# A block of output products that keeps its sums in a retired token buffer, with the scalings of v moved into it

## The chip, the cores and the metric

One core of one Trainium2 chip runs the kernel. Times are device microseconds (us) of one launch; the profile is one more execution, recorded by the hardware profiler, with a span of its own.

## The reference, cut to what matters

```python
# q, k, v: (8, 8, 576, 64); x: (4608, 512); w1, w2: (512, 1024); w3: (1024, 1024); w_out: (1024, 512)
scores = q @ k.T / 8                       # per batch and head
ret = scores * gamma_h ** (i - j), i >= j  # causal decay, gamma_h = 1 - 2 ** (-5 - h)
x = ret @ v                                # heads side by side: (8 * 576, 512)
out = ((x @ w1) * (x @ w2)) @ w3 @ w_out   # float32
```

## The kernel before, in words

Attention is done in chunks. Four pairs of batches times five chunks (64, then four of 128 positions) make 20 steps g. A step scales q and v by the decay (`scale`, `scale_blocks`), transposes q and k (`front` on TensorE, `front_blocks` on VectorE), makes scores (`score`), adds to a running state (`state`) and multiplies with v (`pv`), which leaves x transposed, in tiles of 2 x 192 tokens called xT; there are 12 such tiles m.

The feed-forward part works with seven products in the place of eight (Strassen's scheme). `up` makes a and b of 384 tokens, and their product goes into a tile named `ab` (128 x 16 x 192 values, two buffers in the pool `ffn`). w3 and w_out are multiplied into w3o once. `down` takes a pair of tiles of 128 tokens and multiplies them with w3o: products 1, 7, 2, 6, 5, 4, 3 in this order, four matmul steps each; product 2 goes on in the PSUM bank of product 1, and product 3 in that of product 5.

The order of every engine's work is written out by hand. A `down` block does this (lines of the kernel before):

- It takes an output tile `ot` (L640), 128 x 2 x 2 x 256 values, from a pool with ONE buffer. So the first write of a block waits until the stores of the block that last had this buffer have landed.
- After product 1, ScalarE copies the bank into `ot` (L679); product 2 waits for this copy, since it goes on in that bank. Once `open_second` has been run, the copy goes to another buffer (`cc` or `ra` in the profile).
- After product 6 VectorE adds into `ot` (L695), and ScalarE copies the finished first quadrant (L696). `plus` (L649) adds products 7, 5, 4 and 3. Product 3 waits for the addition of product 5.
- `put` and `store` (L723) send finished rows to HBM, from ScalarE's queue. A DMA issue stands in ScalarE's order like any other instruction.
- After each addition `plus` runs one entry of the list `spread` (sums of weights and their sends to HBM) or, when that is empty, of `pieces` (sums of tokens for the next part), and, except after that of product 3, one entry of the list `aside`. With `ahead`, a block puts the three sums S3, S2 and S1 of the next block (L614, L618, L620) at the end of `aside`.

Around the change three such blocks follow each other. Block 1 is `down((1,0),(1,1))`, in the last step of the loop `first_pair` and after it. Then come `pv(2*NC-1)`, the load and the scaling of v for the step after it (`scale(g + 1, "v", True)`: eight ScalarE instructions, L202, one for each head), and `open_first`, which starts the next sends and loads of weight forms. Block 2 is `down((2,2),(3,2))`, then `open_second` is run, and block 3 is `down((3,0),(3,1))`, with the scaling of q in `aside`. Then `front(10)` transposes k and q (L218), with copies on ScalarE (L221), `state` (L255) and `score` (L233) follow, and a long stage of two-level products (`up2`, L1053) begins. It reads weight forms from three buffers `ra`, filled from `kept` tensors in HBM (L954), which the sends (L895, L898, L901) had written in pieces during the three blocks. The first two fills of `ra` are issued by SP.

Transfers issued by SP and ScalarE share eight completion counters. In the built program, an issue first waits until the transfer that last used the same counter has landed. So a store on ScalarE can wait for a send of SP.

Of the kernel before, what the change touches and what calls it, by code (L numbers as in the profile page):

```python
# [8 lines left out]
F32 = mybir.dt.float32  # L9
# [10 lines left out]
def kernel(  # L20
# [16 lines left out]
    B, H, S, D = q.shape  # L37
    DM = H * D
    DF = moe_w3.shape[0]
    CV = 512  # L40
    P = 128
# [12 lines left out]
    TB = S // NB  # L54
    NT = 2 * TB // P
    KD = DM // P
    KF = DF // P
# [6 lines left out]
    ffn = ctx.enter_context(tc.tile_pool(name="ffn", bufs=2))  # L64
# [6 lines left out]
    pools = {}  # L71
# [123 lines left out]
    def scale(g, nm, scalar=False, engine=nc.gpsimd):  # L195
        c = g % NC
        sz = sizes[c]
        t, gam = live[nm, g], {"q": gq, "v": gk}[nm]
        t = t[:sz].rearrange("p (b h) d -> p b h d", b=2)
        if scalar:  # L200
            for h in range(H) if scalar is True else scalar:
                nc.scalar.mul(t[:, :, h, :], t[:, :, h, :], gam[:sz, c, h:h + 1])  # L202
            return
        engine.tensor_tensor(
            out=t, in0=t, in1=gam[:sz, c].unsqueeze(1).unsqueeze(3).to_broadcast([sz, 2, H, D]), op=ALU.mult)
# [366 lines left out]
    aside, owed, spread, beside, loads = [], [], [], [], []  # L572
    g = 0
# [31 lines left out]
    def pair_of(x, y):  # L605

        if (x, y) not in pairs:
            X, Y = tokens(*x), tokens(*y)
            a = {"A11": X[:, :NP], "A12": X[:, NP:], "A21": Y[:, :NP], "A22": Y[:, NP:],
                 "S3": Y[:, :NP], "S4": X[:, NP:]}  # L610

            def sums(nm):
                if nm == "S3":
                    nc.vector.tensor_tensor(out=a["S3"], in0=a["A11"], in1=a["A21"], op=ALU.subtract)  # L614
                elif nm == "S2":
                    forms = pools["forms"].tile([P, 2, NP, P], F32, tag="forms", name="forms")
                    a["S1"], a["S2"] = forms[:, 0], forms[:, 1]
                    nc.vector.tensor_tensor(out=a["S2"], in0=a["A22"], in1=a["S3"], op=ALU.subtract)  # L618
                else:
                    nc.vector.tensor_tensor(out=a["S1"], in0=a["S2"], in1=a["A11"], op=ALU.add)  # L620
                done.append(nm)

            done = []
            pairs[x, y] = a, done, [lambda nm=nm: sums(nm) for nm in ("S3", "S2", "S1")]
        return pairs[x, y]

    def ahead(x, y, n=3):
        todo_sums = pair_of(x, y)[2]
        for _ in range(min(n, len(todo_sums))):
            aside.append(todo_sums.pop(0))  # L630

    def down(x, y, then=None, last=False):
        a, done, left = pair_of(x, y)
        second = "first" in live
        early = second or last or g >= 2 * NC - 1
        ahead(x, y)
        while len(done) < (1 if second else 3):
            aside.pop(0)()
        ps = {}
        ot = pools["ot"].tile([P, 2, 2, DM // 2], F32, tag="ot", name="ot")  # L640

        def product(nm, A, B, on=None):
            ps[nm] = ps[on] if on else acc.tile([P, DM // 2], F32, tag="acc", name="po")
            for f in range(NP):
                nc.tensor.matmul(ps[nm], a[A][:, f, :], live["W"][B][:, f, :], start=(f == 0 and not on),  # L645
                                 stop=(f == NP - 1), skip_group_check=True)

        def plus(nm, to, sb):
            nc.vector.tensor_add(ot[:, to[0], to[1]], ps[nm], ot[:, sb[0], sb[1]])  # L649
            if spread:  # L650
                spread.pop(0)()
            elif pieces:
                pieces.pop(0)()
            if early and aside and nm != 3:
                aside.pop(0)()

        def put(m, t, row, half=slice(0, 2)):

            i, n = every[m]
            r0 = t * P  # L660
            while r0 < (t + 1) * P:
                b = r0 // TB
                e = min((b + 1) * TB, (t + 1) * P)
                r = (2 * i + b) * S + n * TB + r0 - b * TB
                stores.append((out[r:r + e - r0, half.start * DM // 2:half.stop * DM // 2],
                               ot[r0 - t * P:e - t * P, row, half].rearrange("p h d -> p (h d)")))
                r0 = e
            if not keep_stores and not second:
                store()

        C11, C12, C21, C22 = (0, 0), (0, 1), (1, 0), (1, 1)
        product(1, "A11", "B11")
        first = ot[:, 0, 0]
        if second and not steps[0]:
            first = live["spare"]
        elif second:
            first = live["first"].pop(0)
            live["first"].append(first)
        nc.scalar.copy(first, ps[1])  # L679
        if second:  # L680
            store()
            finish()
            if steps[0] and sent[0] < steps[0] + 3:
                next_forms()
        product(7, "S3", "T3")
        if second:
            multiply()
        while len(done) < 3:
            aside.pop(0)()
        if then:  # L690
            ahead(*then)
        product(2, "A12", "B21", on=1)
        nc.vector.tensor_tensor(out=a["S4"], in0=a["A12"], in1=a["S2"], op=ALU.subtract)
        product(6, "S2", "T2")
        nc.vector.tensor_add(ot[:, 0, 1], ps[6], first)  # L695
        nc.scalar.copy(ot[:, 0, 0], ps[2])  # L696
        if early:
            put(*x, 0, slice(0, 1))
            store()
        plus(7, C21, C12)  # L700
        product(5, "S1", "T1")
        plus(5, C22, C21)
        product(4, "A22", "-T4")
        plus(4, C21, C21)
        put(*y, 1)
        if second:
            store()
        product(3, "S4", "B22", on=5)
        while aside and not early:
            aside.pop(0)()  # L710
        plus(3, C12, C12)
        put(*x, 0, slice(1 if early else 0, 2))
        if last:
            store()
        while aside:
            aside.pop(0)()
# [3 lines left out]
    def store(engine=nc.scalar):  # L720
        while stores:

            engine.dma_start(*stores.pop(0))  # L723
# [125 lines left out]
    ahead((2, 0), (2, 1), 1)  # L849
    up(0, 2, NQ - 1)  # L850
    down((2, 0), (2, 1), ((0, 0), (0, 1)))
    carry(2, 2)
    weights_part.close()
# [6 lines left out]
    keep_stores.clear()  # L860
    store()
    todo = [(down, (0, 0), (0, 1)), (down, (0, 2), (1, 2))]


# [85 lines left out]
    def next_forms(engine=nc.gpsimd):  # L950
        n = sent[0]
        if n < 14 * len(groups):
            nm = NAMES.index(OPERANDS[order[n % 7]][0])
            engine.dma_start(ring[n % 3], kept[n % 14 // 7][nm])  # L954
            sent[0] += 1
# [57 lines left out]
    def finish():  # L1013
        while behind:
            behind.pop(0)()

    def multiply(most=2 * len(order)):
        while results and most:
            gr, h, f, b, z, s = results.pop(0)
            m = groups[gr][s]  # L1020
            if ("ab", *every[m]) not in live:
                live["ab", *every[m]] = ffn.tile([P, 2 * KF, TB], F32, tag="ab", name="ab")
            ab = live["ab", *every[m]].rearrange("p (q i) t -> p q i t", i=4)[:, 2 * h:2 * h + 2, 2 * f + b, :]
            v = z.rearrange("p (m s) w t -> p m s w t", s=2)[:, :, s]
            nc.vector.tensor_mul(ab, v[:, :, 0, :], v[:, :, 1, :])  # L1025
            if s == 0:
                free.append(z)
            most -= 1

    def up2(gr, n):  # L1030
# [88 lines left out]
        behind.append(rest)  # L1119

    real = (up, up2, down)

    def add_group(gr):
# [4 lines left out]
    def work(n):  # L1128
        while n > 0 and todo:
            fn, *args = todo.pop(0)  # L1130

            nxt = next((x for x in todo if x[0] in real), None)
            if nxt and nxt[0] is down:
                if fn is down:
                    args.append(nxt[1:])
                else:
                    ahead(*nxt[1:], 1 if fn is up2 else 3)
            if g == G and not todo:
                fn(*args, last=True)
            else:  # L1140
                fn(*args)
            n -= 1
            while todo and todo[0][0] not in real:
                todo.pop(0)[0]()

    g = NC
# [49 lines left out]
    g = 2 * NC - 1  # L1196
# [3 lines left out]
    pv(g)()  # L1200
    load(g + 2, "v", nc.scalar)
    load(g + 2, "k")
    scale(g + 1, "v", True)
    open_first()
    token_forms(0)

    g = 2 * NC
    work(1)
    aside.append(lambda: scale(g, "q", True))
    work(1)  # L1210
# [55 lines left out]
    g = G  # L1266
# [44 lines left out]
```

## Time and profile before

| what | value |
|---|---|
| median of 3 runs | 835.94 us (835.65 to 836.12) |
| the profiled execution: its own time | 834.5 us |
| the profiled execution: span | 832.8 us |
| TensorE busy in the span | 814.8 us, 98% |
| VectorE, ScalarE, GpSimd busy | 546.3, 291.6, 216.3 us |
| window 335 to 365 us, TensorE busy | 26.59 of 30 us |
| window 335 to 365 us, DMA | share 1.10, 304 GB/s |
| window 400 to 800 us, TensorE busy | 398.04 of 400 us |

In the views, PE is TensorE, PEld its weight loads, DVE VectorE, ACT ScalarE, POOL GpSimd, SP SyncE; a q after an engine's name is its queue, where DMAs are issued. A line of the timeline gives the start, the length, the engine, the line of the kernel, the operation with tiles out<-in, the number of instructions, and in brackets the idle time before it with what ended it. A DMA share of one means that 16 DMA engines had packets all the time (packets overlap, so it can be a little over one).

### The profile page before, as it was taken

What the parts mean: (1) busy time and instruction counts of PE and PEld (TensorE: products, weight loads), DVE (VectorE), ACT (ScalarE), POOL (GpSimd) and SP (SyncE); (2) the same over time, 40 slices, a digit from 0 to 9 for tenths busy, and PEclk for the clock granted to TensorE, in tenths of its full rate; (3) what the DMA queues carried; (4) which work ended last, traced back from release to release, by engine and by line L of the source; (5) the groups of instructions that cost most, each with busy time, mean ns of one, the idle gap of its engine ahead of it and who ended that gap; (6) DMA issues with size and microseconds to landing.
All of it is one profiled execution on the core that took longest, in us unless ns stands there. A gap on an engine that the chain in (4) does not pass through costs nothing.

```text
span 832.8 us, 15818 instructions
## 1 busy us (share of the span) xinstructions
PE 814.8 (98%) x6117; PEld 733.5 (88%) x6117; DVE 546.3 (66%) x962; ACT 291.6 (35%) x609; POOL 216.3 (26%) x247
## 2 busy tenths in 40 slices
PE   7999999999999999999999999999999999999998
PEld 7888999644888998789999889998889998899987
DVE  4899999992554558754657755677745667646653
ACT  4787566581111010245443024341034331033300
POOL 1000000001103262005556005565006460045600
PEclk9999999999999999999999999999999999999999
DMA  9995464436045568998886447978245453145311
GB/s 195 228 215 138 78 153 127 123 105 112 3 80 130 86 175 276 286 282 209 202 227 184 100 85 205 232 232 222 56 92 180 162 191 114 37 150 215 138 30 46
DMA packets 197485, 126.96 MB, mean 152 GB/s; under 512 B 157849, under 2 KB 179097, under 8 KB 197409
## 3 DMA queue, kind: packets, MB, share of 16 engines
q1 hardware_dynamic: 168560, 50.40, 29.4%
q0 software_dynamic: 11824, 63.31, 23.4%
q10 hardware_dynamic: 17024, 12.23, 5.3%
q8 instruction: 48, 0.79, 0.4%
q14 instruction: 29, 0.23, 0.1%
HBM read 103.62 MB, written 22.28 MB: 151 GB/s over the span
## 4 chain that ended last, share of the span: by engine, by line
PE 81%; DVE 7%; DMA 5%; SPq 3%; issue 2%; ACT 2%; POOL 0%; ACTq 0%; DVEq 0%
PE po L645 21%; PE up L1053 17%; PE up L528 14%; PE seed L1053 13%; PE ps L477 7%; PE xps L299 3%; PE sc L233 3%; PE xps L274 1%; DMA out_dram<-ot 1%; PE st L255 1%; SPq L171 1%; DMA bl_k<-in_k_dram 1%; DVE ab L1025 1%; PE tp L218 1%; DMA kept<-wA 1%
## 5 line engine op out<-in xcount | busy, mean ns | idle before, releaser
L645 PE MATMUL po<-w3o,ab 128*128 128x256 f32 x552 | 125.4, 381 | 3.3 <-DVE ot L649 2.4
L645 PEld LDWEIGHTS po<-w3o,ab 128*128 128x128 f32 x552 | 103.6, 190 | 20.4 <-DVE ot L649 4.8
L1058 POOL TENSOR_TENSOR cc<-cc 128x384 f32<-128x384 f32 x112 | 109.3, 1002 | 3.8 <-ACT cc L1076 2.4
L1065 DVE TENSOR_TENSOR cc<-seed,cc 128x384 f32<-128x384 f32 x88 | 48.7, 553 | 69.1 <-PE seed L1053 60.1
L1053 PE MATMUL up<-xT,ra 128*128 128x192 f32 x384 | 73.6, 328 | 0.4 <-DMA ra<-kept 0.4
L181 POOL TENSOR_TENSOR bl_q<-bl_q,gqs 128x512 f32<-128x512 f32 (+1 forms) x26 | 26.0, 1020 | 184.1 <-DMA bl_q<-in_q_dram 180.5
L528 PE MATMUL up<-xT,wA 128*128 128x192 f32 x384 | 70.8, 328 | 0.3 <-ACT xT L306 0.3
L533 DVE TENSOR_TENSOR c<-up,c 128x384 f32<-128x384 f32 x80 | 44.0, 551 | 38.9 <-PE up L528 38.6
L1065 DVE TENSOR_TENSOR cc<-up,cc 128x384 f32<-128x384 f32 x88 | 48.5, 551 | 29.8 <-PE up L1053 21.8
L236 DVE TENSOR_TENSOR pm<-sc,mask 128x512 f32<-128x512 f32 (+1 forms) x80 | 45.3, 628 | 33.4 <-PE sc L233 33.3
L1053 PEld LDWEIGHTS up<-xT,ra 128*128 128x128 f32 x384 | 63.7, 190 | 1.7 <-DMA ra<-kept 0.7
L645 PE MATMUL po<-wB,forms 128*128 128x256 f32 x288 | 65.1, 379 | 0.0
L528 PEld LDWEIGHTS up<-xT,wA 128*128 128x128 f32 x384 | 63.3, 190 | 1.8 <-issue 0.7
L645 PEld LDWEIGHTS po<-wB,forms 128*128 128x128 f32 x288 | 54.7, 190 | 7.4
L1072 ACT COPY seed<-up 128x384 f32<-128x384 f32 x56 | 25.9, 463 | 100.1 <-PE up L1053 59.2
L954 POOL DMA_DIRECT2D ra<-kept x53 | 29.9, 565 | 117.7 <-PE seed L1053 88.5
L477 PE MATMUL ps<-wo,w3T 128*128 128x512 f32 x128 | 55.1, 592 | 0.0
L1053 PE MATMUL up<-ra 128*128 128x192 f32 x288 | 54.8, 326 | 0.0
L1053 PE MATMUL seed<-e,ra 128*128 128x192 f32 x256 | 50.9, 329 | 0.0
L477 PEld LDWEIGHTS ps<-wo,w3T 128*128 128x128 f32 x128 | 24.3, 190 | 30.1 <-issue 29.7
L1053 PEld LDWEIGHTS up<-ra 128*128 128x128 f32 x288 | 48.1, 190 | 0.1
L528 PE MATMUL up<-T,wS 128*128 128x192 f32 x256 | 46.7, 326 | 1.3 <-ACT e L395 1.3
(129 smaller groups left out, 1463.8 us busy)
## 6 DMA issues: line engine op xcount, KB each, us to landing
ra<-kept POOLq DMA_DIRECT2D x53, 896.0 KB, 5.1
raw<-in_moe_w_dram SPq DMA_DIRECT2D x72, 128.0 KB, 3.0
out_dram<-ot ACTq DMA_DIRECT2D x50, 128.0 KB, 2.3
bl_q<-in_q_dram SPq DMA_DIRECT2D x192, 32.0 KB, 3.3
bl_k<-in_k_dram SPq DMA_DIRECT2D x136, 32.0 KB, 3.2
raw<-in_moe_w_dram SPq DMA_DIRECT2D x16, 256.0 KB, 6.1
ld_k<-in_k_dram SPq DMA_DIRECT2D x8, 512.0 KB, 6.3
raw<-in_moe_w_out_dram SPq DMA_DIRECT2D x32, 128.0 KB, 2.7
```

The costliest lines, as they stand in the source:

```text
L181: nc.gpsimd.tensor_tensor(out=part, in0=part, in1=gqs[:, :, n0:n0 + n].unsqueeze(3).to_broadcast([P, NP, n, BL]), op=ALU.mult)
L233: nc.tensor.matmul(sc[j][:sz, p, :sz], kT[hs, b, p, :sz], qT[hs, b, p, :sz], start=True, stop=True)
L236: nc.vector.tensor_mul(pm[:sz, b, j, :, :sz], sc[j][:sz, :, :sz], mask[:sz, :sz].unsqueeze(1).to_broadcast([sz, NP, sz]))
L477: nc.tensor.matmul(ps, live["w3T", ft][:, g, :], live["wo"][:, g, :], start=(g == 0), stop=(g == KF - 1))
L528: nc.tensor.matmul(ps[:, w, :], a[:, w, r, :], b[:, r, :], start=(new and w == r == 0), stop=(w == r == 1), skip_group_check=True)
L533: nc.vector.tensor_add(c[:, to], ps, c[:, sb])
L645: nc.tensor.matmul(ps[nm], a[A][:, f, :], live["W"][B][:, f, :], start=(f == 0 and not on), stop=(f == NP - 1), skip_group_check=True)
L954: engine.dma_start(ring[n % 3], kept[n % 14 // 7][nm])
L1053: nc.tensor.matmul(ps[:, w, :], weight_of(slot, a, w), B[b], start=(new and w == 0), stop=True, skip_group_check=True)
L1058: nc.gpsimd.tensor_tensor(out=o, in0=o, in1=i, op=ALU.add)
L1065: nc.vector.tensor_add(c[:, j], ps, with_add[:, j])
L1072: nc.scalar.copy(p6, p1)
```

## The change

Two edits. The output tile of block 2, the one called with x == (2, 2), is no longer taken from the one-buffer pool; a buffer of the pool `ffn` with the tag `ab` is taken, under the name `spare`, and its first 2048 values a partition are used in the shape of `ot`. With the order in which the two `ab` buffers are handed out, it is the one that held the tokens of block 1. The scaling of v for step 10 is no longer ahead of block 2; it is put into `aside` in two halves of four heads, so that it runs after the additions of products 7 and 5 of block 2.

```diff
@@ down
-        ot = pools["ot"].tile([P, 2, 2, DM // 2], F32, tag="ot", name="ot")
+        if x == (2, 2):
+
+            ot = ffn.tile([P, 2 * KF, TB], F32, tag="ab", name="spare").rearrange("p f t -> p (f t)")
+            ot = ot[:, :2 * DM].rearrange("p (r c d) -> p r c d", r=2, c=2)
+        else:
+            ot = pools["ot"].tile([P, 2, 2, DM // 2], F32, tag="ot", name="ot")
@@ main order
     load(g + 2, "k")
-    scale(g + 1, "v", True)
     open_first()
     token_forms(0)
 
     g = 2 * NC
+    aside.extend(lambda j=j: scale(g, "v", range(j, j + H // 2)) for j in (0, H // 2))
     work(1)
     aside.append(lambda: scale(g, "q", True))
     work(1)
```

## The prediction

> **What bounds the kernel now.** The page comes first: is there one engine that sets the time?
>
> ```profile
> span 832.8 us, 15818 instructions
> PE 814.8 (98%) x6117; PEld 733.5 (88%) x6117; DVE 546.3 (66%) x962; ACT 291.6 (35%) x609; POOL 216.3 (26%) x247
> ```
>
> TensorE is busy for 98% of the span, so only its idle time can be won, and only where the change acts. I then read TensorE's timeline for the three blocks.
>
> ```profile
> 338.97 1.99 PE L645 MATMUL po<-w3o,carry 128*128 128x256 f32 x8 [1.40 <-ACT ot L679]
> ...
> 346.66 1.99 PE L645 MATMUL po<-w3o,carry 128*128 128x256 f32 x8 [0.52 <-DVE ot L649]
> ...
> 360.67 1.99 PE L645 MATMUL po<-w3o,ab 128*128 128x256 f32 x8 [1.31 <-DVE ot L649]
> ```
>
> Three stalls: product 2 of block 2 (1.40 us), product 3 of block 2 (0.52), product 3 of block 3 (1.31), together 3.23 us. That is all this stretch has to give. Why they are there, the timelines of VectorE and ScalarE tell.
>
> ```profile
> 357.59 0.42 DVE L695 TENSOR_TENSOR ot<-po,cc 128x256 f32<-128x256 f32 x1 [2.68 <-DMA out_dram<-ot]
> ```
>
> ```profile
> 336.21 2.45 ACT L202 ACTIVATE ld_v<-ld_v,gk 64x128 f32<-64x128 f32 x8
> 338.56 0.36 ACT L679 COPY ot<-po 128x256 f32<-128x256 f32 x1
> ...
> 362.85 1.12 ACTq L723 DMA_DIRECT2D out_dram<-ot  x2
> 364.01 0.65 ACT L221 COPY kT<-tp 128x256 f32<-128x256 f32 x2 [1.34 <-PE tp L218]
> 364.54 0.67 ACT L221 COPY qT<-tp 128x256 f32<-128x256 f32 x2
> ```
>
> Stall one: the copy L679 stands behind eight scalings of v. Stall three: block 3's first addition waits until block 2's last store has landed, since both use the one `ot`. The last three lines matter for what comes next: ScalarE issues block 3's two stores of the lower rows and only then copies kT and qT, which the scores need. Last, the DMA, in the table of windows:
>
> ```profile
> 335.00:365.00 30.00, 26.59 (x158) 21.92 (x157) 21.89 (x38) 8.22 (x26) 0.03 (x1) 1.00 1.10 304
> ```
>
> The share is 1.10 over the whole stretch: the transfers are saturated beside all this.
>
> [...] the stores of L723 at 362.85 show 1.12 us, but ScalarE's copies are held until these are out, at 363.97. [...] for SP's queue: sends issued at 350.93, 354.63, 357.57 and 359.69 landed after 7.2, 7.8, 5.2 and 4.6 us, so at 358.2, 362.4, 362.8 and 364.3, in order. [...] the granted clock is 1.00 in all windows, and no gap of this stretch exceeds 1.40 us.
>
> **Part 1, the scalings moved.** Removed ahead of L679: eight of L202, 2.45 us together. The copy of product 1 now goes to the spare buffer, needs no store to have landed, and follows the xT copies that end at 336.33. It ends near 336.7, before product 7 ends at 337.55. So product 2 starts near 337.55: stall one is gone, minus 1.40. The scalings come after ScalarE's first store of block 2. In the built program this store waits for the counter of the v load issued at 335.36, which takes 7.7 us, so until 343.0; the scalings then run to 346. Their reader, `state`, was at 363.7. Cost nothing, under a cover of 17 us; without it 2.45 us. The load of v isn't moved.
>
> **Part 2, `aside` reordered.** Two scalings now stand ahead of the sums S3, S2, S1. VectorE's order becomes: addition of 7, weight sums (1.22 + 0.95), additions of 5 and 4, three token sums (2.01), S3, addition of 3, two sums of 0.95, S2, S1. Before, S3 (0.69) stood ahead of the addition of 5. From L695 near 341.4: the addition of 5 starts near 344.2 and ends at 344.6; product 4 ends at 344.7. So stall two is gone, minus 0.52. S3 ends near 347.9 and the addition of 3 at 348.2, when product 7 of block 3 wants S3 and its bank (product 1 of block 3 ends near 348.4). S2 and S1 end at 350.6 and 351.2, wanted at 352.1 and 353.9. Cost nothing; slack 0.2 us at the tightest.
>
> **Part 3, the buffer.** Block 3 takes `ot` again, whose last stores are those of block 1; they were out before the copy at 338.56. So L695 of block 3 no longer waits 2.68 us. It follows product 6, at 354.1; the addition of 5, behind sums of 0.95 and 1.02, ends near 357.0, and product 4 ends at 357.5. Stall three is gone, minus 1.31. The spare buffer had block 1's tokens, all read when product 3 of block 1 ended, at 331.0, and in the built program the copy into it waits for product 1 alone; it is next written by products near 385, with its stores landed. Cost nothing. No transfer and no arithmetic is added or taken away.
>
> **Sum up to here:** block 3 ends at 362.6 - 3.2 = 359.4.
>
> **Part 4, what is late next.** TensorE transposes k and q (1.2 us) and does `state` (1.15), to about 361.8. Then scores need qT. Before, scores began at 364.99, 0.98 us after the kT copies began (364.01), with TensorE fed until then. ScalarE reaches the stores of the lower rows earlier now, but these wait for counters. In the built program of before the two wait for the fifth and the sixth send of the second half's weight forms, in the new one for the fourth and the fifth. The fifth is the one issued at 357.57 and landed 5.2 us later, at 362.8. It stands in SP's queue behind 2.7 MB or more (a fill of `ra`, 896 KB; four sends of 256 KB, one of 768 KB), all under a saturated DMA, so an earlier issue gains it nothing. What changes its landing: block 3's stores are earlier [...]. The first was under way before as well; one of 128 KB is new ahead of it. At 304 GB/s that is 0.43 us, an upper bound; the lower is nothing, or a gain of 0.2 if the earlier stores of block 2 fill the one weak microsecond at 345 (DMA share 0.78, 211 GB/s in the table of windows). I take +0.2: 363.0. Then 0.1 to the issue, about 0.5 for it (1.12 for two), and kT begins near 363.6 in the place of 364.01. Gain 0.4, bounds 0.0 to 0.7. The scores then begin at 364.6 and TensorE idles about 2.8 us ahead of them: of the 3.2, 2.8 come back as one new wait.
>
> **After that.** The second step of the long stage needs the second fill of `ra`, issued at 364.51 when the last send of weights had landed, and in 5.1 us later, at 369.6. TensorE wanted it at 371.5, so it had 1.9 us of cover. With one to three stores (128 to 384 KB, 0.4 to 1.3 us at 304 GB/s) now ahead of the last send it comes at 370.0 to 370.9, and is wanted at 371.1: it just holds, and would stop any gain above 0.6 to 1.9. From 365 to the end TensorE's waits add up to 2.0 us, none on absolute times; counters and orders are the same again after the first block loads, so the 0.4 goes through.
>
> **Sum.** Span 832.8 - 0.4 = 832.4; with the 1.7 around it 834.1 against the profiled 834.5. The median shown is 1.44 above that execution: 835.94 - 0.4 = 835.5 us. Within 0.2% (1.67 us), about what a measurement of this kernel can tell from no change.
>
> **Rivals.**
> (a) *No wait takes the stalls' place*: the sends land early enough. 835.94 - 3.2 = 832.7. For it: ScalarE is idle and the sums are done. Against it: the share of 1.10. Chance 0.05.
> (b) *The counter wait ends earlier, the second fill of `ra` is the next limit*: gain 0.8 to 1.9, so 834.0 to 835.1; I take 1.4, 834.5. It needs the fifth send in by 362. [...] Against: the order of landing. Chance 0.16, a third of it past 0.2%.
> (c) *Slower: [...] halves the clock.* Place: between `state` and the scores. [...] Chance 0.10.
> (d) *The change doesn't do what it says*, since the buffer handed out is still read: the time of before, 835.9. Against it is the end of its readers at 331.0 (part 3). Chance under 0.01.
>
> **Numbers.** Main case 0.69, own range 835.2 to 836.0. Faster by over 0.2%: 0.05 from (a), 0.05 from (b), 0.03 for a landing of sends that I have wrong by more than its bounds: 0.13. Slower by over 0.2%: 0.06 from (c), [...] 0.04 for a wait not seen here: 0.10. Within: 0.77. For 8 in 10 the range takes most of (b) and the mild half of (c): 834.1 to 836.9.
>
> **What would show it.** Right: no stall ahead of products 2 and 3 in blocks 2 and 3; L695 of block 3 near 354; one TensorE gap of 2 to 3 us ahead of L233, on ScalarE's qT or kT copy; these right behind the stores of L723, which wait for a send of weights landed near 363. Wrong: the copies come by 362, and the gap is small (a, b); or PEclk falls under 1 after 364 (c); or one of the three stalls stays.

## The result and the profile after

The changed kernel takes 837.08 us (median of 22 runs, 836.24 to 841.32), the kernel before, run beside it, 835.66 us (22 runs): a ratio of 1.0018, 95% interval 1.0010 to 1.0027. The forecast was 835.5. The time went 1.4 us up and not 0.4 down, and lies 0.2 us over the top of the range. Single runs of one kernel spread over 4 us or so here. TensorE's clock has a part in that: the two longest runs of the changed kernel, 841.32 and 841.11 us, have the lowest mean clock, 0.990. The mean granted clock was 0.996 or less in 15 of the 22 runs of the changed kernel, and in 21 of 128 runs of the kernel before that were taken beside the experiments; it was 0.999 or more in none of the 22, and in 72 of the 128. A mean doesn't tell where the clock fell. The profiled execution of the changed kernel took 836.71 us and has a mean clock of 0.996.

The page after: span, engines, and the row of the granted clock in 40 slices.

```profile
span 835.0 us, 15819 instructions
PE 816.9 (98%) x6117; PEld 736.2 (88%) x6117; DVE 544.9 (65%) x962; ACT 291.6 (35%) x609; POOL 216.3 (26%) x247
PEclk9999999999999999989999999999999999999999
```

One slice has an 8 in the clock's row; before there was none. The rest of the kernel is the same, so the stretch of the three blocks is looked at again. TensorE's timeline (lines after block 1 have moved down by five in the code):

```profile
337.89 1.89 PE L650 MATMUL po<-w3o,carry 128*128 128x256 f32 x8
...
344.89 1.99 PE L650 MATMUL po<-w3o,carry 128*128 128x256 f32 x8
...
357.08 1.89 PE L650 MATMUL po<-w3o,ab 128*128 128x256 f32 x8
358.90 0.71 PE L218 MATMUL tp<-ident,ld_k 64*128 64x64 f32 x8
359.45 0.66 PE L218 MATMUL tp<-ident,ld_q 64*128 64x64 f32 x8
360.04 1.15 PE L255 MATMUL st<-ld_v,ld_k 64*64 64x64 f32 x32
364.54 1.97 PE L233 MATMUL sc<-qT,kT 64*64 64x64 f32 x32 [3.36 <-ACT qT L221]
366.44 2.93 PE L1046 MATMUL seed<-w3o,ident 128*128 128x384 f32 x4
```

The first three lines had brackets before (1.40, 0.52, 1.31 us); now they have none, and block 3 ends at 358.9. More was won than these 3.23 us. Two windows, the first of the kernel before and the second of the changed one, go from the first product of block 2 to the first transpose (columns: window, length, then busy time and count of PE, PEld, DVE, ACT, POOL, then granted clock, DMA share and GB/s):

```profile
333.85:362.59 28.74, 25.44 (x114) 20.87 (x113) 20.70 (x35) 7.15 (x22) 0.00 (x0) 1.00 1.11 303
334.33:358.90 24.57, 24.57 (x114) 20.98 (x113) 20.89 (x35) 7.36 (x22) 0.00 (x0) 1.00 1.12 295
```

The same matmuls are through in 24.57 us in the place of 28.74, so 4.17 us sooner: 3.30 us of idle time are gone, and 0.87 us of what was shown as busy. Then TensorE waits 3.36 us for qT. Before, the scores, the matmuls after them (into a tile named `seed`) and the first matmuls of the second step of the long stage were

```profile
364.99 1.15 PE L233 MATMUL sc<-qT,kT 64*64 64x64 f32 x32
366.07 1.56 PE L1041 MATMUL seed<-w3o,ident 128*128 128x384 f32 x4
...
371.53 0.81 PE L1053 MATMUL up<-xT,ra 128*128 128x192 f32 x4
```

Now the scores take 1.97 us for the same 32 matmuls, and the four into `seed` 2.93. What ScalarE did meanwhile:

```profile
360.79 2.73 ACTq L728 DMA_DIRECT2D out_dram<-ot  x2
363.56 0.65 ACT L221 COPY kT<-tp 128x256 f32<-128x256 f32 x2 [8.15 <-DMA out_dram<-ot]
364.09 0.39 ACT L221 COPY qT<-tp 128x256 f32<-128x256 f32 x1
364.35 0.35 ACTq L959 DMA_DIRECT2D ra<-kept  x1
```

ScalarE does no work for 8.15 us, in part because it stands at two stores; the second is held until 363.05. In the built program it waits there for the fifth send of weights, which SP issued at 357.93 and whose last write landed at 363.03. The table of windows, with the same columns, tells why the work after the gap is slow:

```profile
360.00:362.00 2.00, 1.18 (x34) 1.01 (x32) 1.86 (x6) 0.00 (x0) 0.58 (x1) 1.00 1.08 385
362.00:364.00 2.00, 0.00 (x0) 0.00 (x0) 0.00 (x0) 0.44 (x2) 0.00 (x0) 0.99 1.11 355
364.00:366.00 2.00, 1.46 (x28) 1.46 (x30) 0.31 (x1) 1.33 (x4) 0.00 (x0) 0.50 1.05 280
366.00:368.00 2.00, 2.00 (x13) 1.28 (x10) 1.18 (x4) 0.00 (x0) 0.00 (x0) 0.50 0.86 330
368.00:370.00 2.00, 2.00 (x6) 1.39 (x5) 0.00 (x0) 0.00 (x0) 0.00 (x0) 0.50 1.05 438
370.00:372.00 2.00, 2.00 (x12) 1.93 (x11) 0.00 (x0) 0.94 (x2) 0.00 (x0) 0.81 0.73 159
```

The clock is at half from just before 364 to nearly 371, and at once when the work comes back. From the scores to the first matmul of the second step of the long stage it is 9.36 us (364.54 to 373.90), before 6.54 (364.99 to 371.53): 2.82 us. Block 2 began 0.48 us later in this execution than in the one of before (334.33 against 333.85), so the scores came 0.93 us earlier than before, counted from there. 2.82 - 0.93 = 1.9 us are lost at the second step; with the 0.48 of the later start that is 2.4, and the spans differ by 2.2.

There is a second thing, in the view of single DMA issues. These are the two fills of `ra` for the second and the third step, of the changed kernel (columns: KB each, us to landing):

```profile
ra<-kept ACTq DMA_DIRECT2D x1, 896.0 KB, 8.5
ra<-kept SPq DMA_DIRECT2D x1, 896.0 KB, 8.6
```

Before, SP's fill was out 0.48 us ahead of ScalarE's and was in after 5.1 us, at 369.6. Now the two start at 364.38 and 364.35, and both land near 373. The second step is wanted at 373.9 with the clock as it is, so here nobody waits. With the full clock it would have been wanted near 371 (an estimate: 364.54 and the 6.54 us of before). So there are two suspects: **the clock** (theory A) and **the fills that share the transfers** (rival B).

### The profile page after: what moved, and what is told of

It reads as the page before. It is cut to its first block, busy times and chain, and to the rows that moved or that the text cites. A ratio compares the mean times of both kernels' runs of the same rounds, so it can differ in the third digit from the quotient of the medians.

```text
span 835.0 us, 15819 instructions
## 1 busy us (share of the span) xinstructions
PE 816.9 (98%) x6117; PEld 736.2 (88%) x6117; DVE 544.9 (65%) x962; ACT 291.6 (35%) x609; POOL 216.3 (26%) x247
## 4 chain that ended last, share of the span: by engine, by line
PE 87%; DMA 5%; DVE 4%; SPq 2%; issue 1%; ACT 1%; POOL 0%; ACTq 0%; DVEq 0%
PE po L650 23%; PE up L1058 17%; PE up L528 14%; PE seed L1058 13%; PE ps L477 7%; PE sc L233 4%; PE xps L299 4%; PE xps L274 2%; PE st L255 1%; DMA ld_q<-in_q_dram 1%; PE tp L218 1%; SPq L171 1%; DMA raw<-in_moe_w_dram 1%; DMA bl_k<-in_k_dram 1%; DVE ab L1030 1%
```

## The experiments

Ten kernels, each timed beside the kernel before, whose median was 835.73 to 835.91 us then. The ratio is not the quotient of the two medians and can differ from it by 0.1% (the buffer alone).

| run | median us | ratio to before (95%) | wait ahead of scores in the profile, us | halved clock after 360 in the profile |
|---|---|---|---|---|
| changed kernel | 837.08 | 1.0018 (1.0010 to 1.0027) | 3.36 | 6.8 us |
| buffer alone | 836.72 | 1.0002 (0.9990 to 1.0015) | 0.39 | 6.8 us |
| scaling alone | 836.97 | 1.0017 (1.0010 to 1.0023) | 2.06 | 6.8 us |
| gap filled | 839.17 | 1.0033 (1.0020 to 1.0046) | none | 3.4 us, later |
| stores late | 833.30 | 0.9977 (0.9968 to 0.9986) | none | none |
| gap filled, fills in order | 835.67 | 0.9996 (0.9989 to 1.0003) | none | none |
| fills in order | 836.87 | 1.0012 (1.0002 to 1.0022) | 3.21 | 3.4 us |
| stores late, fills in order | 833.35 | 0.9967 (0.9955 to 0.9980) | none | none |
| before, stores late | 835.78 | 0.9990 (0.9978 to 1.0002) | none | none |
| stores late, S sends behind the fill | 833.86 | 0.9984 (0.9968 to 0.9999) | none | none |
| gap half filled, fills in order | 835.68 | 0.9999 (0.9984 to 1.0014) | 1.38 | none |

### One part alone

The buffer alone: the two edits of the main order are undone.

```diff
+    scale(g + 1, "v", True)
     open_first()
@@
-    aside.extend(lambda j=j: scale(g, "v", range(j, j + H // 2)) for j in (0, H // 2))
     work(1)
```

> The spare buffer alone; the scaling of v stays ahead of block 2. Theory A (TensorE's clock: the new gap of 3.36 us ahead of the scores halves the clock for some 7 us): stalls one and two (1.40 and 0.52 us) stay, stall three goes, so TensorE reaches the scores only about 1.3 us earlier, the gap is 1.0 to 2.0 us, PEclk stays 1.00 everywhere, and the time is that of before within 0.5 us. Rival B (the fills of ra: ScalarE's third fill is now issued beside SP's second one, both land near 373, 3.4 us later than the second one before, and the second step of the long stage waits for it): that step begins near 373 whatever the clock does, the time is 1 to 1.5 us over before.

Measured: 836.72 us; the median is 1.0 us higher, but the runs spread from 834.14 to 839.13, and by the interval no change is shown. Stalls one and two stay (1.44 and 0.53), stall three is gone. TensorE's timeline of this run, and the 3.41 us ahead of the fall (half as long as the slow clock lasted):

```profile
363.37 0.27 PE L218 MATMUL tp<-ident,ld_q 64*128 64x64 f32 x1 [0.31 <-ACT ld_q L202]
363.96 0.52 PE L218 MATMUL tp<-ident,ld_q 64*128 64x64 f32 x5 [0.31 <-ACT ld_q L202]
...
366.20 1.98 PE L233 MATMUL sc<-qT,kT 64*64 64x64 f32 x32 [0.39 <-ACT qT L221]
```

```profile
361.72:365.13 3.41, 2.64 (x42) 2.01 (x42) 3.08 (x9) 2.19 (x8) 0.58 (x1) 1.00 0.85 262
```

The clock fell to half at 365.13, with two gaps of 0.31 us in the 3.41 us ahead of it; the one of 0.39 came after the fall. Both theories missed: A said that the clock would stay at 1.00, and B that the second step would begin near 373 (it began at 375.46, with no wait for its fill). So A's idle gap is not what makes the clock fall here. Nine of 21 runs had a mean clock of 0.997 or less.

The scaling alone: the same two edits made in the kernel before.

> The scaling of v moved alone; block 2 keeps the one output buffer. Stalls one and two go (1.9 us), block 3 waits again for block 2's last store, which is issued 2 us earlier. Theory A (clock): gap ahead of the scores 1.5 to 3.0 us, PEclk 1.00, time within 0.5 us of before[...]. Rival B (fills): second step near 373, 1 to 1.5 us over before with PEclk 1.00.

Measured: 836.97 us, 0.17% over before, though stall two and stall three are gone (block 2's last store is out earlier, by itself) and 1.08 of stall one stays (the copy still needs block 1's last store). The gap is 2.06 us, with 1.96 us busy in the 3.41 us ahead of the fall, and the clock fell to half at 363.83 all the same; B's wait didn't show. So the shorter gap doesn't save the clock, and this part alone has the whole loss (1.0017, beside 1.0018 for both parts).

### The gap filled

```diff
     state(g)
+    keep_busy(13)
     score(g)
```

> The changed kernel with 13 matmuls of no use (ident by ident, in an own PSUM tile) between the state and the scores, some 3.1 us, which fill the gap. Theory A (clock): PEclk 1.00 after 364, scores at 364.5 as in the changed kernel, the long stage begins near 367 and not at 369.2, time 0.4 us under before (835.3). Rival B (fills): PEclk 1.00, but the second step of the long stage waits some 2 us for its fill of ra, landing near 373, and the time is 1 us over before (836.7).

Measured: 839.17 us, a ratio of 1.0033 beside 1.0018 for the changed kernel; the intervals touch, so it is no better, and whether it is worse isn't shown.

```profile
365.30 1.15 PE L233 MATMUL sc<-qT,kT 64*64 64x64 f32 x32
...
374.51 0.89 PE L1058 MATMUL up<-xT,ra 128*128 128x192 f32 x4 [2.50 <-DMA ra<-kept]
```

```profile
374.00:376.00 2.00, 1.49 (x9) 1.52 (x10) 0.00 (x0) 0.46 (x1) 0.00 (x0) 0.95 0.15 24
376.00:378.00 2.00, 2.00 (x8) 2.00 (x7) 0.00 (x0) 0.96 (x2) 0.27 (x1) 0.50 0.43 66
```

The scores run at full clock (1.15 us), and then TensorE waits 2.50 us for the second fill, as B has it; within 2 us of the end of this new gap the clock falls after all, to 0.50 from 376 to 378. In six of the 11 runs the mean clock was 0.999 or more; they took 836.97 to 839.34 us, all over the 835.73 of before. So the wait for the fill is enough by itself to take the gain: B is right too, hidden in the changed kernel behind the slow clock.

### The fills in order, with the gap filled and without

```diff
     front(g)
-    next_forms(nc.scalar)
+    next_forms(nc.sync)
```

> The changed kernel with the 13 matmuls of no use in the gap, and the third fill of ra issued by SP behind the second, not by ScalarE beside it. If the clock and the shared fills are the two costs and no other is there: second fill lands at 369.5 to 370.5, the second step of the long stage waits under 0.5 us, PEclk 1.00 after 364 in most runs, time 0.2 to 0.6 us under before (835.3). If something else costs: 836.5 or more, as in the changed kernel.

> The changed kernel with the third fill of ra on SP behind the second, and nothing else. Clock theory: the gap of 3.4 us and the halved clock stay, TensorE wants the second fill later than it lands in either order, the time is that of the changed kernel within 0.5 us (836.6 to 837.1). Fill theory: second fill lands 3 us earlier, time 0.5 us or more below the changed kernel, 836.0 or less.

Measured: 835.67 and 836.87 us. The first, with both costs taken away:

```profile
364.55 1.15 PE L233 MATMUL sc<-qT,kT 64*64 64x64 f32 x32
...
371.10 0.81 PE L1058 MATMUL up<-xT,ra 128*128 128x192 f32 x4
```

The two fills, both issued by SP, take 7.0 us in the median, no wait for them is left, and from the scores to the second step it is 6.55 us, as before the change. The two together make up for the loss, to the kernel before within 0.11% (the expected gain of 0.2 to 0.6 us is inside the interval and not shown). The second, with the fills in order alone:

```profile
364.81 1.97 PE L233 MATMUL sc<-qT,kT 64*64 64x64 f32 x32 [3.21 <-ACT qT L221]
...
372.85 0.81 PE L1058 MATMUL up<-xT,ra 128*128 128x192 f32 x4
```

The second step has no wait for its fill: with the slow clock the order of the fills gives nothing that can be measured (the intervals overlap), as A has it. The four cases, as ratios to before: gap open and fills sharing 1.0018, gap open and fills in order 1.0012, gap filled and fills sharing 1.0033, gap filled and fills in order 0.9996. One cost taken away alone brings nothing; both must go.

### The stores behind the copies

This tests the gap's own cause. Block 3 leaves its lower stores in the list, and they are issued after the copies of kT and qT.

```diff
         put(*y, 1)
-        if second:
+        if second and x != (3, 0):
             store()
@@
     front(g)
+    store()
     next_forms(nc.scalar)
```

> The changed kernel with the stores of the lower rows of block 3 issued by ScalarE behind the copies of kT and qT. If these stores' wait is what made the gap, the copies come at 359.6 to 361 and the scores begin near 361.3 with no gap over 0.5 us; the first step of the long stage begins near 364. Then the second fill of ra is next. Theory A: it lands near 370, a wait of 1 to 2 us, clock 1.00, time 1.0 to 1.9 us under before. Rival B: second and third fill share, land near 373, the wait is 4 to 5 us, the clock falls too, and the time is 1 to 2.5 us over before.

> The changed kernel with block 3's lower stores behind the copies of kT and qT and the third fill on SP. The wait of 1.00 us on ScalarE's seed copy (ScalarE stood in the issue of the third fill) goes, and the second step then waits longer for the second fill, which lands at 369.5 or so at best: time equal to the run with the late stores alone within 0.6 us (832.8 to 833.4). If the second fill weren't what ends that wait, 832.0 or less.

> The kernel before with block 3's lower stores behind the copies of kT and qT, and nothing else. TensorE comes to the scores at 364.9 there and had no gap ahead of them, so kT and qT 0.8 us earlier give nothing: 835.7, within 0.3 us of before. If the late stores were good by themselves (for instance by their effect on the fills), 834.5 or less.

Measured: 833.30 us with the change, 833.35 with the third fill on SP as well, and 835.78 in the kernel before. ScalarE's timeline of the first, then TensorE's:

```profile
359.65 0.65 ACT L221 COPY kT<-tp 128x256 f32<-128x256 f32 x2 [3.98 <-PE tp L218]
```

```profile
366.15 0.92 PE L1058 MATMUL seed<-e,ra 128*128 128x192 f32 x4 [1.00 <-ACT seed L1077]
...
370.10 0.89 PE L1058 MATMUL up<-xT,ra 128*128 128x192 f32 x4 [1.08 <-DMA ra<-kept]
```

The copies follow the transposes at once, there is no gap ahead of the scores, and the stalls' gain comes through until the second fill stops it. ScalarE's fill goes out at 364.76 here, and the wait for SP's ends at 370.10. With the third fill on SP:

```profile
365.75 0.92 PE L1058 MATMUL seed<-e,ra 128*128 128x192 f32 x4 [0.63 <-ACT seed L1077]
...
370.47 0.89 PE L1058 MATMUL up<-xT,ra 128*128 128x192 f32 x4 [1.85 <-DMA ra<-kept]
```

The wait on ScalarE shrinks by 0.37 us and the wait for the fill grows by 0.77: the same limit, and the same time. In the kernel before, the late stores by themselves give nothing that can be measured. So the change is worth about 2 us once these stores are out of the way: 2.4 by the medians (835.78 to 833.35), 1.9 by the ratios (0.9990 to 0.9967). These two kernels are faster than both the kernel before and the changed one.

One more, to move that limit: the sends of the second half's S forms (1.15 MB) go behind the second fill, which reads other forms. The middle of the edit, with the rest left out (`late_sends` is the list of these sends, and the lines on `ring` and `next_forms` stood lower before):

```diff
         ring.extend([ra[:, :FORM], ra[:, FORM:2 * FORM]])
+        next_forms(nc.sync)
+        for f in late_sends:
+            f()
         cs = wp.tile([P, 2, 4, 2, TB], F32, tag="wS1", name="cc")
```

> The run with late stores and the third fill on SP, and in addition the sends of the second half's S forms (1.15 MB) behind the second fill of ra, which doesn't need them. If that fill is what ends the wait of 1.85 us ahead of the second step, it lands near 366 to 367, the wait is under 0.3 us, and the time is 1.2 to 1.8 us below that run: 831.6 to 832.2. If the wait has another cause, 833.3 as before.

Measured: 833.86 us, no gain. The wait ahead of the second step is 1.15 us and not under 0.3; the step begins at 369.12, and before this edit at 370.47. The third fill is late in turn, by 1.02 us. TensorE's waits in this run:

```profile
369.12 0.89 PE L1069 MATMUL up<-xT,ra 128*128 128x192 f32 x4 [1.15 <-DVE cc L1081]
374.93 0.92 PE L1069 MATMUL up<-ra 128*128 128x192 f32 x4 [1.02 <-DMA ra<-kept]
```

The first line's wait is put down to VectorE; whether the fill came last there is not shown. Traffic was moved and not removed. That these sends are what slows the fill is argued, not shown by a run.

### Half the gap

> The run with 13 matmuls in the gap and the third fill on SP, with 6 matmuls in the place of 13: an idle gap of 1.5 to 1.9 us is left, about the longest stall of the kernel before. [...]

```diff
-    keep_busy(13)
+    keep_busy(6)
```

Two readings are tested, neither shown by the runs so far. The length of the one gap decides: then the clock stays at 1.00 and the time is 835.4 to 835.9 us. Or the little work around it decides too: then the clock falls in part of the runs and the median is 836.0 to 836.9.

Measured: 835.68 us, 0.9999 (0.9984 to 1.0014). In the profile 1.38 us of gap are left and the clock stays (1.00 from 363.19 to 366.60); the mean clock was 0.996 or less in 5 of 14 runs. The fall is not certain and not excluded, and a fall elsewhere counts in that mean: this profile's is 0.998, with the scores and the matmuls into `seed` at the lengths of full clock (1.15 and 1.56 us). This one doesn't decide between the two readings.

## Why the forecast was wrong, point by point

- **Stalls one, two and three** (minus 1.40, 0.52, 1.31): right in cause, and none is left in the profile after. But "That is all this stretch has to give" is wrong: it gave 4.17 us and not 3.23. A bracket doesn't hold all that a stall costs, since 0.87 us of busy time went with the three. VectorE's addition in block 3 was forecast for 354.1:

```profile
353.88 0.42 DVE L700 TENSOR_TENSOR ot<-po,cc 128x256 f32<-128x256 f32 x1 [1.09 <-PE po L650]
```

- **Costs put at nothing** (the scalings, the new order of sums, the buffer): right. The scalings end at 346.2, and no sum holds TensorE by more than 0.1 us.
- **The new wait of Part 4**: right in place and cause. The kT copies were forecast for 363.6 and came at 363.56, behind the stores that wait for the fifth send; with the stores elsewhere the wait is gone. Mis-sized is the landing of that send, put at 0.2 us later: counted from the start of block 2, ScalarE's second store was held until 28.7 us, and the send had landed at 28.9 before, so it was free 0.2 us earlier, which was the other bound. The gain at the scores was 0.93 us and not 0.4, counted that way; that 363.56 hits 363.6 so well is luck, as this execution began block 2 0.48 us later. The new wait was put at 2.8 us and is 3.36: counted from block 2, TensorE was done with the state 1.1 us sooner than forecast (26.9 us, not 28.0), the scores began only 0.5 sooner (30.2, not 30.75).
- **Rival (c), the clock**: this is where it went wrong. I gave 0.10 to the clock, on the grounds that a wait of 2.8 us was too short for it, which no trace of before shows. The gap was 3.36, and that isn't what mattered: the clock fell with a gap of 2.06 too, and with two of 0.31. What failed is the step that took a length of idle time as the condition, and with it "the 0.4 goes through". The price is measured: the way from the scores to the second step took 2.82 us longer, with half clock for 6.83 us.
- **The second fill of ra**: the step "it just holds" failed too. I let it be late by the stores ahead of it (0.4 to 1.3 us). That ScalarE's fill would now go out beside it was put at nothing, without a word. The two fills, issued 0.03 us apart, share, and the second landed 3.4 us later than before. In the changed kernel this is hidden by the slow clock; with the clock held it is a wait of 2.50 us.
- **The sum without the two**: with the two failed steps taken away by experiment, the kernel is at 0.9996 of before (0.9989 to 1.0003), where the forecast's 0.4 us would be 0.9995. That fits the forecast, and it fits no gain as well.

Shown by runs: that the gap comes from the stores on ScalarE, that the slow clock and the shared fills are each enough to take the gain, and that no third cost over about 0.7 us is there (1.0003 at most, against 0.9995). Open: what makes the clock fall, and in only a part of the runs of the kernel before, and whether the kind of work matters to it. Open too: why a start 0.48 us later keeps the two fills apart and one of 0.03 us doesn't.

In three kernels the half clock began at 363.95 us (changed), 363.83 (scaling alone) and 365.13 (buffer alone), and lasted 6.8 us each. Of the 3.41 us before the fall TensorE was busy for 0.64 us in the changed kernel, for 1.96 with the scaling alone, and for 2.64 with the buffer alone.

## What to carry to other kernels

Before stalls are taken from an engine that is busy 98% of the time, ask which deadlines on the path aren't moved by it (here a send of weights under a DMA share of 1.10, through a completion counter), and put the instructions that the path needs ahead of those that wait for such a deadline. Several small waits drawn together into one can cost more than their sum: here waits of 3.23 us, none of which took the clock down, became one of 3.36 us, after which it was at half for 6.83 us. A cost that an experiment doesn't show may be hidden behind another: take both away before one is called harmless.

## What the runs showed of the hardware that was not expected

- The clock fell with TensorE busy 2.64 of the 3.41 us before (buffer alone), where the work was transposes and matmuls of 64 rows and columns; in the kernel before, 3.40 us with 2.63 us busy (from 359.90), most of it on full 128 x 128 blocks, kept 1.00. Less busy stretches kept it too, one of full blocks (the first line, stores late and fills in order) and one with half the gap and the scores in it (the second, gap half filled):

```profile
367.18:370.60 3.42, 1.57 (x10) 1.31 (x10) 1.02 (x2) 1.59 (x6) 0.00 (x0) 1.00 0.92 353
363.19:366.60 3.41, 2.03 (x36) 1.52 (x36) 1.10 (x4) 1.69 (x5) 0.00 (x0) 1.00 1.07 304
```

  So busy time alone doesn't decide. What does was not shown.
- Half clock lasted 6.8 us in three profiles (both parts, and each part alone) and 3.4 us in two (fills in order, gap filled).
- Two fills of 896 KB, issued on two queues 0.03 us apart, took 8.5 and 8.6 us; with 0.48 us between them 5.1 and 8.5; both on SP's queue (gap filled, fills in order) they took 7.0 us in the median.
